# A scan layer with a gated feed-forward: a small early read of w_up on ScalarE's queue, and one store of the last slab whole

## The chip, the cores and the metric

The kernel runs on one core of one Trainium2 chip. The metric is the device time of one execution in microseconds (us); lower is better. The median of three timed runs before the change is 178.91 us (178.73 to 178.92).

## The reference, cut to what matters

The input x has 2048 tokens of 512 features in bf16. It is normalized per token. One branch is a diagonal complex linear recurrence over the tokens, the other a gated feed-forward of width 1376; the output is x plus their product.

```
xn = layernorm(x)
Lam_bar = exp(exp(log_dt) * (Lambda_re + 1j*Lambda_im))
Bu = xn @ B_bar.T                                   # B_bar from Lambda, B_re, B_im
h[t] = Lam_bar * h[t-1] + Bu[t]                     # 512 complex states
s = 2 * real(h @ C.T) + xn * Dskip
g = silu((gelu(xn @ w_gate) * (xn @ w_up)) @ w_down)
out = x + s * g
```

## The kernel before, in words

The tokens are cut into four slabs of 512, each of four tiles of 128 tokens (one per partition). For each slab TensorE forms the gate and up products (`gate_tile`), the down product (`down_pair`), the input product of the recurrence (`half`) and its output product (`y_part`); VectorE runs the recurrence as scans over rotated states, ScalarE moves products out of PSUM with Gelu, Silu or Copy, and SP's queue issues nearly all transfers: loads, transposes by DMA and stores.

The order of the work isn't found at run time. Every step is added to a plan with its reads and writes (`Plan.add`), and `Plan.run` emits the steps in the order of the tuple `ORDER`, written out by step number. Costs, ranks and due times that stand in the calls were a planner's, and decide nothing here. Each engine executes its own instructions in the order in which they were emitted; an instruction that waits holds all that stand behind it on its queue.

The first slab has a way of its own, since its data are still on their way:

- SP issues tiles 0, 1 and 2 of x (L222), then w_up in four quarters of 128 rows by 1024 columns and the rest of its columns in one piece (L213), tile 3 of x, w_gate in two pieces, and later loads.
- ScalarE loads an activation table with a Silu of one element (L254) and issues three small reads of 512 parameters each: log_dt, Lambda_im and Lambda_re (L256).
- TensorE first multiplies constants into banks that are overwritten later (`dummies` L299, `fill` L303).
- Tile 0 of x is summed over its 512 columns by VectorE (384, L341) and ScalarE (128, L339), and centered by VectorE (L343). Tiles 1 and 2 are summed by ScalarE (L347) and centered by VectorE (L348).
- TensorE transposes tile 0 (L313), tile 1 (L328), then the parameters (L603, L604), then begins the product of tile 0 with w_up (L388), transposes tile 2 (L328), and goes on with the product, one quarter of w_up after the other.

The framework gives every transfer that SP or ScalarE issues one of eight completion semaphores, in turn. The issue of a transfer waits, on the queue that issues it, until the transfer that last held the same semaphore has landed. In the built program the turn is not the order of `ORDER` but that in which the framework expects the issues. It begins like this (the number is the semaphore's):

```
0 x tile 0    1 x tile 1    2 x tile 2        3 log_dt
4 w_up 0      5 Lambda_im   6 w_up 1          7 Lambda_re
0 w_up 2      1 w_up 3      2 w_up, rest      3 x tile 3
4 w_gate      5 w_gate      6 w_down, last    7 x slab 1
0 Dskip       1 ...
```

At the other end, the output of a tile is the recurrence's product times g (L502), plus x (L508), and its store is issued from SP (L513). In the last slab the stores of tiles 0 and 1 are cut into two halves of 256 columns each, that of tile 2 is whole, and tile 3 is worked and stored in two halves. The line `cuts` (L511) decides this.

Of the kernel before, what the change touches and what calls it, by code (L numbers as in the profile page):

```python
# [17 lines left out]
PE, ACT, DVE, POOL, SP = "PE", "ACT", "DVE", "POOL", "SP"  # L18


ORDER = (
# [23 lines left out]
)  # L45


# [33 lines left out]
def kernel(  # L81
# [27 lines left out]
    NS = S // TS  # L109
    M = TS // P  # L110
# [4 lines left out]
    HD = D // 2  # L115
# [5 lines left out]
    V, A, G, T = nc.vector, nc.scalar, nc.gpsimd, nc.tensor  # L121
# [6 lines left out]
    def sb(name, shape, dt=BF16):  # L128
        return consts.tile(shape, dt, name=name)
# [49 lines left out]
    def dve(n, emit, reads=(), writes=(), rate=1.0, base=DV, **kw):  # L179
        return pl.add(DVE, base + n / 960.0 / rate, emit, reads, writes, lag=0.13, **kw)  # L180

    def acts(n, emit, reads=(), writes=(), ptr=0, **kw):
        return pl.add(ACT, AC + 0.12 * ptr + n / 1200.0, emit, reads, writes, lag=0.16, **kw)

    def pe(n, cols, emit, reads=(), writes=(), **kw):
        return pl.add(PE, n * (cols + 6) / 2400.0, emit, reads, writes, lag=0.22, **kw)
# [4 lines left out]
    def dma(eng, issue, land, emit, reads=(), writes=(), **kw):  # L191
        return pl.add(eng, issue, emit, reads, writes, lag=land, **kw)
# [43 lines left out]
    for ri, src in enumerate((A_B_re, A_B_im)):  # L236
        dma(SP, 2.0, 3.0, lambda ri=ri, src=src: nc.sync.dma_start_transpose(out=BT[:, ri, :, :], in_=src), writes=[("BT", ri)],
            after=list(sp_last), svc=TURN)
# [13 lines left out]
    one = nc.const_aps.tensor(1.0, [P, 1], FP32)  # L252

    first = [acts(1, lambda: act(out=tiny[:], in_=one, func=AF.Silu), [], ["tiny"], rank=910.0, not_before=0.72)]  # L254
    for i, (t, v) in enumerate(((pv0[0:4, :], A_log_dt), (pv1[0:4, :], A_Lambda_im), (pv1[4:8, :], A_Lambda_re))):
        first = [dma(ACT, 0.48, 1.7, lambda t=t, v=v: A.dma_start(out=t, in_=v.rearrange("(k p) -> k p", p=P)),  # L256
                     writes=[("pv", i)], rank=900.0, not_before=0.8, after=first)]
# [230 lines left out]
    def y_part(s, m, c0, c1, bank, key, seed, e):  # L488

        w = c1 - c0  # L490
        ps = bank[:, 0:w]
        if seed:
            acts(w, lambda: act(out=ps, in_=sk[s % 2][:, m, c0:c1], func=AF.Copy), [("sk", s % 2, m)], [key])  # L493

        def f():
            for j in range(2 * NPT):
                T.matmul(ps, lhsT=hst[s % 2][:, j // NPT, j % NPT, m * P : (m + 1) * P], rhs=C2[:, j // NPT, j % NPT, c0:c1],  # L497
                         start=(j == 0 and not seed), stop=(j == 2 * NPT - 1), skip_group_check=True)
        pe(2 * NPT, w, f, [("hst", s % 2, 0), ("hst", s % 2, 1)] + C2S + ([key] if seed else []), [key])
        gi, b = g2s[s, m]  # L500
        if seed:
            dve(w, lambda: V.tensor_tensor(out=yg[e][:, c0:c1], in0=ps, in1=g2[gi][:, b, c0:c1], op=ALU.mult), [key, ("g2", gi, b)], [("yg", e, c0)])  # L502
        else:
            ys = tF[:, 0, c0:c1]
            dve(w, lambda: V.tensor_tensor(out=ys, in0=ps, in1=sk[s % 2][:, m, c0:c1], op=ALU.add), [key, ("sk", s % 2, m)], [("tF",)])
            dve(w, lambda: V.tensor_tensor(out=yg[e][:, c0:c1], in0=ys, in1=g2[gi][:, b, c0:c1], op=ALU.mult), [("tF",), ("g2", gi, b)], [("yg", e, c0)])
        o = 2 + m % 2 if s == NS - 1 and m >= M - 2 else m % 2
        dve(w, lambda: V.tensor_tensor(out=ot[o][:, c0:c1], in0=yg[e][:, c0:c1], in1=x_tok[:, s * M + m, c0:c1], op=ALU.add),  # L508
            [("yg", e, c0), ("x", s, m)], [("ot", o, c0)], rate=2.0)
        mg = s * TS + m * P  # L510
        cuts = (0, HD) if (NS - 1, 0) <= (s, m) < (NS - 1, M - 2) else (c0,)  # L511
        for lo, hi in zip(cuts, (*cuts[1:], c1)):
            dma(SP, 0.35, 1.5, lambda lo=lo, hi=hi: nc.sync.dma_start(out=out_td[mg : mg + P, lo:hi], in_=ot[o][:, lo:hi]), [("ot", o, c0)], [("out", s, m, lo)], svc=(2, 0.4, 0.9))  # L513

# [218 lines left out]
    for pt in range(NPT):  # L733
# [3 lines left out]
            out=C2[:, 0, pt, :], in0=CT[:, 0, pt, :], scalar=cre[:, pt : pt + 1], in1=tF[:, 1, :], op0=ALU.mult, op1=ALU.subtract),  # L737
            ["coef", ("CT", 0), ("tF",)], [("C2", 0, pt)], base=0.13)
        dve(512, lambda pt=pt: V.scalar_tensor_tensor(
            out=C2[:, 1, pt, :], in0=CT[:, 1, pt, :], scalar=ncre[:, pt : pt + 1], in1=tF[:, 0, :], op0=ALU.mult, op1=ALU.subtract),  # L740
# [104 lines left out]
```

## Time and profile before

| what | us |
|---|---|
| median of three timed runs | 178.91 |
| lowest and highest | 178.73, 178.92 |
| span of the profiled execution | 176.3 |
| median less that span | 2.6 |
| TensorE busy in the span | 172.3 |
| VectorE busy | 156.9 |
| ScalarE busy | 123.5 |

The span runs from the first to the last instruction of the one execution that the profiler recorded; of that execution no other time is given, so the table sets the median of the timed runs beside it. PE stands for TensorE's products, PEld for its loads of weights, DVE for VectorE, ACT for ScalarE, POOL for GpSimd and SP for SyncE; a q behind the name is the engine's queue, where transfers are issued. L with a number is a line of the kernel before. Times of products overlap, since one starts before the last has ended.

### The profile page before, as it was taken

The numbers are of one execution on the slowest core, as the hardware profiler recorded it, in microseconds if no ns is written. First come the engines' busy times: TensorE is split into PE (matmuls) and PEld (weight loads), VectorE is DVE, ScalarE is ACT, GpSimd is POOL, SyncE is SP. The second block draws the span as 40 slices with busy tenths as digits, with TensorE's granted clock in tenths as the row PEclk, the third lists the DMA queues.
The fourth block names the chain that finished last, engine by engine and source line by source line (L and its number), as shares of the span: only waits on it lengthen the run. The fifth ranks groups of instructions, "written<-read, shape, count | busy, mean of one in ns | idle before, by whom it ended". The sixth has DMA issues, their size and how long they took to land.

```text
span 176.3 us, 2421 instructions
## 1 busy us (share of the span) xinstructions
PE 172.3 (98%) x847; PEld 82.3 (47%) x847; DVE 156.9 (89%) x252; ACT 123.5 (70%) x236; POOL 11.2 (6%) x25
## 2 busy tenths in 40 slices
PE   8999999999999999999999999999999999999992
PEld 2555454444454544444455454444444455444451
DVE  3859999999699984999979999899999999999764
ACT  6599979969999999799588845383058518482240
POOL 2660030000200000000040000000000000000000
PEclk9999999999999999999999999999999999999999
DMA  5999999998000809422000084194000007627112
GB/s 156 322 371 225 205 226 260 219 279 137 0 0 12 188 20 192 95 75 46 0 0 6 30 137 95 41 182 86 0 0 0 0 30 162 65 41 154 45 58 76
DMA packets 48355, 18.66 MB, mean 106 GB/s; under 512 B 40312, under 2 KB 47832, under 8 KB 48344
## 3 DMA queue, kind: packets, MB, share of 16 engines
q1 hardware_dynamic: 48320, 18.52, 48.8%
q8 instruction: 6, 0.10, 0.3%
q14 instruction: 5, 0.04, 0.1%
q10 hardware_dynamic: 24, 0.00, 0.0%
HBM read 6.46 MB, written 2.10 MB: 49 GB/s over the span
## 4 chain that ended last, share of the span: by engine, by line
PE 97%; DVE 1%; issue 0%; DVEq 0%
PE ring L449 32%; PE ring L481 22%; PE ring L547 16%; PE ybank L497 15%; PE ring L418 5%; PE ring L388 3%; PE ybank L418 2%; PE ring L299 1%; DVE yg L502 1%; PE ybank L299 1%; DVE junk L508 1%; PE ybank L328 0%; PE ring L303 0%; PE ring L313 0%; PE ring L603 0%
## 5 line engine op out<-in xcount | busy, mean ns | idle before, releaser
L449 PEld LDWEIGHTS <-xnT 128*128 128x128 bf16 x288 | 28.2, 98 | 28.4
L481 PE MATMUL ring<-wd,atT 128*128 128x512 bf16 (+1 forms) x176 | 39.3, 379 | 0.0
L449 PE MATMUL ring<-wg,xnT 128*128 128x512 bf16 (+1 forms) x144 | 31.6, 357 | 0.0
L449 PE MATMUL ring<-wu,xnT 128*128 128x512 bf16 (+1 forms) x144 | 31.3, 357 | 0.0
L547 PE MATMUL ring<-xnT,BT 128*128 128x512 bf16 x128 | 30.1, 379 | 0.0
L578 DVE TENSOR_TENSOR_SCAN Fs<-rho,ini,W 128x512 bf16<-128x512 f32 x24 | 29.7, 1271 | 0.1
L452 ACT ACTIVATE ub<-ring 128x512 bf16<-128x512 f32 (+1 forms) x36 | 19.2, 555 | 13.8 <-PE ring L449 13.7
L497 PE MATMUL ybank<-C,hst 128*128 128x512 bf16 x120 | 27.7, 379 | 0.0
L481 PEld LDWEIGHTS <-atT 128*128 128x128 bf16 (+1 forms) x176 | 17.2, 97 | 20.9
L549 ACT ACTIVATE U<-ring 128x512 bf16<-128x512 f32 x32 | 18.1, 599 | 7.5 <-PE ring L547 7.5
L452 ACT ACTIVATE gt<-ring 128x512 bf16<-128x512 f32 (+1 forms) x36 | 19.5, 556 | 3.7 <-PE ring L449 3.5
L497 PEld LDWEIGHTS <-hst 128*128 128x128 bf16 x136 | 13.3, 98 | 14.0
L484 ACT ACTIVATE g<-ring 128x512 f32<-128x512 f32 x16 | 9.4, 594 | 14.3 <-PE ring L481 14.2
L547 PEld LDWEIGHTS <-BT 128*128 128x128 bf16 x128 | 12.5, 97 | 14.8
L559 DVE TENSOR_TENSOR Q<-U,tab 128x4096 bf16<-128x4096 bf16 x8 | 18.3, 2289 | 0.9 <-ACT tab L646 0.7
L559 DVE TENSOR_TENSOR Q<-Fs,tab 128x4096 bf16<-128x4096 bf16 x8 | 18.3, 2288 | 0.1
L502 DVE TENSOR_TENSOR yg<-ybank,g 128x512 bf16<-128x512 f32 x15 | 10.2, 685 | 5.8 <-PE ybank L497 5.7
L763 ACT ACTIVATE junk<-x_tok 128x512 bf16<-128x512 bf16 x16 | 10.0, 632 | 1.2 <-DMA x_tok<-in_A_x_dram 1.2
L493 ACT ACTIVATE ybank<-sk 128x512 f32<-128x512 bf16 x15 | 9.1, 605 | 1.7 <-DVE yg L502 1.6
L768 ACT ACTIVATE xna<-x_tok,nb,rs 128x512 bf16<-128x512 bf16 x12 | 9.5, 812 | 0.0
L578 DVE TENSOR_TENSOR_SCAN Fs<-rho,W 128x512 bf16<-128x512 f32 x8 | 9.3, 1210 | 0.1
L458 DVE TENSOR_TENSOR at<-gt,ub 128x1024 bf16<-128x1024 bf16 x12 | 8.2, 683 | 0.0
(140 smaller groups left out, 169.7 us busy)
## 6 DMA issues: line engine op xcount, KB each, us to landing
x_tok<-in_A_x_dram SPq DMA_DIRECT2D x3, 512.0 KB, 4.6
out_dram<-ot SPq DMA_DIRECT2D x12, 128.0 KB, 1.8
wd<-in_B_w_down_dram SPq DMA_DIRECT2D x1, 1280.0 KB, 7.1
wu<-in_B_w_up_dram SPq DMA_DIRECT2D x4, 256.0 KB, 3.9
wg<-in_B_w_gate_dram SPq DMA_DIRECT2D x1, 864.0 KB
x_tok<-in_A_x_dram SPq DMA_DIRECT2D x4, 128.0 KB, 2.1
wg<-in_B_w_gate_dram SPq DMA_DIRECT2D x1, 512.0 KB, 6.0
wu<-in_B_w_up_dram SPq DMA_DIRECT2D x1, 352.0 KB, 5.3
```

What stands on the lines that cost most here:

```text
L418: T.matmul(ps[:, 0 : b - a], lhsT=lhs(k), rhs=wt[:, k, a:b], start=(k == 0), stop=(k == KT - 1))
L449: T.matmul(ps[:, 0 : b - a], lhsT=xnT[:, s % 2, m, k, :], rhs=wt[:, k, a:b], start=(k == 0), stop=(k == KT - 1))
L452: acts(b - a, lambda: act(out=dst[:, a:b], in_=ps[:, 0 : b - a], func=AF.Copy if up else AF.Gelu_apprx_tanh), [("bank", r)], [key], table= ...
L481: T.matmul(ps[:], lhsT=atT[:fs, k, m * P : (m + 1) * P], rhs=wd[:fs, k, :], start=(k == 0), stop=(k == NFT - 1))
L497: T.matmul(ps, lhsT=hst[s % 2][:, j // NPT, j % NPT, m * P : (m + 1) * P], rhs=C2[:, j // NPT, j % NPT, c0:c1], start=(j == 0 and not seed ...
L502: dve(w, lambda: V.tensor_tensor(out=yg[e][:, c0:c1], in0=ps, in1=g2[gi][:, b, c0:c1], op=ALU.mult), [key, ("g2", gi, b)], [("yg", e, c0)])
L547: T.matmul(ps[:], lhsT=BT[:, ri, k, pt * P : (pt + 1) * P], rhs=xnT[:, s % 2, :, k, :], start=(k == 0), stop=(k == KT - 1))
L549: acts(512, lambda q=q, ri=ri, ps=ps: act(out=U[ui][:, ri, q, :], in_=ps[:], func=AF.Copy), [("bank", r)], [("U", ui, q, ri)])
L559: dve(4096, lambda: V.tensor_tensor(out=Qf, in0=src.unsqueeze(1).to_broadcast(WQ), in1=table, op=ALU.mult), reads, ["Q"], rate=2.0)
L578: pl.add(DVE, 1.12 if s == 0 else 1.185, lambda ri=ri, q=q, pt=pt, first=first: V.tensor_tensor_scan(out=Fs[:, ri, q, :], data0=rho[:, pt ...
L763: acts(512, lambda i=i, fn=fn, sc=sc, m=m: act(out=junk()[:], in_=x_tok[:, s * M + m, :], func=fn, scale=sc, accum_out=sx[:, s, i, m : m + ...
L768: acts(512, lambda m=m: act(out=xn[m], in_=x_tok[:, s * M + m, :], func=AF.Identity, scale=rs[:, s, m : m + 1], bias=nb[:, s, m : m + 1]), ...
```

## The change

A new step stands between the one-element Silu and the parameters. It reads w_up (512 rows of 1376) at every eighth row, the first 32 columns: 16 partitions with four pieces of 32 bf16 values each, 64 pieces of 64 bytes. Nothing reads the tile that it fills. The condition on the cut of stores now begins at tile 1 of the last slab, so the store of tile 0 is whole. The numbers in `ORDER` are shifted by the new step and by the missing store; otherwise the sequence of steps is the same, with the new step second, behind the Silu.

```
     first = [acts(1, lambda: act(out=tiny[:], in_=one, func=AF.Silu), [], ["tiny"], rank=910.0, not_before=0.72)]
+    seen = sb("seen", [16, 4, 32])
+    first = [dma(ACT, 0.48, 1.7, lambda: A.dma_start(out=seen[:], in_=B_w_up.rearrange("(a b) f -> a b f", a=16)[:, 0:32:8, 0:32]),
+                 writes=["seen"], rank=900.0, not_before=0.8, after=first)]
     for i, (t, v) in enumerate(((pv0[0:4, :], A_log_dt), (pv1[0:4, :], A_Lambda_im), (pv1[4:8, :], A_Lambda_re))):
...
-        cuts = (0, HD) if (NS - 1, 0) <= (s, m) < (NS - 1, M - 2) else (c0,)
+        cuts = (0, HD) if (NS - 1, 1) <= (s, m) < (NS - 1, M - 2) else (c0,)
```

In the built program the semaphores are given in this turn:

```
0 x tile 0    1 x tile 1    2 x tile 2        3 the new read
4 w_up 0      5 log_dt      6 w_up 1          7 Lambda_im
0 Lambda_re   1 w_up 2      2 w_up 3          3 w_up, rest
4 x tile 3    5 w_gate      6 w_gate          7 w_down, last
0 x slab 1    1 Dskip       2 ...
```

The last transfers, from the halves of tile 1 on, have the same semaphores as before.

46 rows, old and new, of the table ORDER are left out of this document.

## The prediction, as it stood before the result

> **What bounds the kernel now.** I read the page's busy shares and its chain first, then the busy time by stretches, then the order of time up to 6 us and from 169 us. The page:
>
> ```profile
> PE 172.3 (98%) x847; PEld 82.3 (47%) x847; DVE 156.9 (89%) x252; ACT 123.5 (70%) x236; POOL 11.2 (6%) x25
> ...
> PE 97%; DVE 1%; issue 0%; DVEq 0%
> ```
>
> TensorE is busy 98% of the span and makes up 97% of the chain that ended last. The busy time by stretches (stretch, its length, then busy time and count of each engine) tells where the other few per cent lie:
>
> ```profile
> 5.00:30.00 25.00, 25.00 (x131) 12.43 (x130) 22.13 (x64) 21.00 (x41) 7.19 (x14) 1.00 1.09 274
> 30.00:60.00 30.00, 30.00 (x149) 14.28 (x147) 27.96 (x39) 27.85 (x56) 1.01 (x1) 1.00 0.61 115
> ...
> 150.00:171.30 21.30, 21.30 (x102) 9.81 (x101) 18.34 (x23) 9.84 (x19) 0.00 (x0) 1.00 0.37 71
> 171.30:176.30 5.00, 1.75 (x17) 1.32 (x14) 2.37 (x6) 0.00 (x0) 0.00 (x0) 1.00 0.26 79
> ```
>
> In the stretches shown up to 171.30 TensorE's busy time equals the length to the last digit, at the full granted clock (1.00). So from 5 us on nothing is waited for, and the end is the moment at which this unbroken run begins, plus a constant, plus the tail. The change touches exactly these two ends: the first 5 us, and stores of the last slab. What sets the beginning is in the chain by pieces and in the order of time (start, length, engine, line; in brackets the idle time before and what ended it):
>
> ```profile
> 4.50 0.40 PE ybank L328 x4
> 4.90 0.11 PE ring L603
> 5.01 0.03 PE ring L604
> 5.03 0.55 PE ring L388 x2
> ```
>
> ```profile
> 0.72 1.28 ACT L254 ACT_TABLE_LOAD   x1 [0.72 <-PEq L829]
> 0.79 0.55 ACTq L256 DMA_DIRECT2D pv<-in_A_log_dt_dram  x1
> 1.38 0.26 ACTq L256 DMA_DIRECT2D pv<-in_A_Lambda_im_dram  x1
> 1.66 0.31 ACTq L256 DMA_DIRECT2D pv<-in_A_Lambda_re_dram  x1
> 2.85 0.31 ACT L339 ACTIVATE junk<-x_tok 128x128 bf16<-128x128 bf16 x1 [0.63 <-DMA x_tok<-in_A_x_dram]
> 3.06 0.19 ACT L339 ACTIVATION_READ_ACCUMULATOR junk<-x_tok 128x1 f32 x1
> 3.33 0.63 ACT L347 ACTIVATE junk<-x_tok 128x512 bf16<-128x512 bf16 x1
> 3.52 0.41 DVE L343 TENSOR_SCALAR xna<-x_tok,ma,mb 128x512 bf16<-128x512 bf16 x1
> 3.87 0.19 ACT L347 ACTIVATION_READ_ACCUMULATOR junk<-x_tok 128x1 f32 x1
> 3.96 0.63 ACT L347 ACTIVATE junk<-x_tok 128x512 bf16<-128x512 bf16 x1
> 4.09 0.35 DVE L348 TENSOR_SCALAR xna<-x_tok,ma 128x512 bf16<-128x512 bf16 x1 [0.16 <-ACT junk L347]
> 4.50 0.23 PEld L328 LDWEIGHTS <-xna 128*128 128x128 bf16 x4 [0.23 <-DVE xna L348]
> 4.83 0.17 PE L603 MATMUL ring<-ident,pv 4*128 4x4 bf16 x1
> 5.65 4.91 PE L388 MATMUL ring<-wu,W 128*128 128x512 bf16 x22
> ```
>
> The reader is to see one path: tile 1 of x lands, ScalarE sums it (L347, 3.33), VectorE centers it (L348, 4.09), TensorE transposes it (L328, 4.50), then the parameters (L603, L604), then the first product with w_up (L388, 5.03). L328 is the last place at which the weight queue waited (0.23). The first quarter of w_up must be there for L388 too. The issues on SP's queue and the time to landing of single loads (the last number) say whether it is:
>
> ```profile
> 0.72 1.34 SPq L222 DMA_DIRECT2D x_tok<-in_A_x_dram  x3
> 2.11 2.33 SPq L213 DMA_DIRECT2D wu<-in_B_w_up_dram  x5
> 4.49 0.50 SPq L222 DMA_DIRECT2D x_tok<-in_A_x_dram  x1
> 5.04 1.49 SPq L213 DMA_DIRECT2D wg<-in_B_w_gate_dram  x2
> ```
>
> ```profile
> x_tok<-in_A_x_dram SPq DMA_DIRECT2D x1, 128.0 KB, 2.1
> ```
>
> ```profile
> wu<-in_B_w_up_dram SPq DMA_DIRECT2D x1, 256.0 KB, 2.8
> ```
>
> ```profile
> wu<-in_B_w_up_dram SPq DMA_DIRECT2D x1, 256.0 KB, 3.3
> ```
>
> ```profile
> wu<-in_B_w_up_dram SPq DMA_DIRECT2D x1, 256.0 KB, 4.5
> ```
>
> x tile 0 is issued at 0.72 and lands 2.1 later, at 2.82. The first quarter of w_up is issued at 2.11 and lands at 4.91, ahead of its use at about 5.0 by a tenth or less. Issues of w_up are 0.47 apart (2.33 for five), so the second goes out at 2.58 and lands at 5.88, needed at 5.65 + 2 x 0.216 = 6.08 (a product takes 4.75 / 22 = 0.216 in the chain; 4.91 here counts the last one's tail). The third goes out at 3.05 and lands at 7.55, needed after ten products at 7.81. So w_up is near the limit three times, and late nowhere.
>
> **The change part by part.** *The read itself.* It is the first transfer on ScalarE's queue, so the three parameter reads move back by one place. It moves 64 x 64 bytes = 4 KB, against 128 KB of the tile of x that is under way. Nobody waits for its data. If its purpose is that later reads of w_up start faster, the gain is bounded: DMA rates are
>
> ```profile
> 3.30:4.10 0.80, 0.80 (x5) 0.23 (x4) 0.53 (x4) 0.77 (x3) 0.00 (x0) 1.00 0.89 247
> 4.10:5.00 0.90, 0.90 (x13) 0.55 (x12) 0.82 (x4) 0.90 (x4) 0.00 (x0) 1.00 1.00 319
> ```
>
> 247 GB/s while w_up starts and 319 after. The loss is 0.80 x (1 - 247/319) = 0.18 us, which I take as the most that the stream of w_up can come forward. TensorE has at most about 0.1 to gain from it, and only if tile 1 of x comes earlier too, since L328 to L604 fill 4.50 to 5.03. I count it at 0.
>
> *ScalarE's queue.* Each issue of the parameters takes 0.26 to 0.55; the read's own I put at the first one's 0.55 (bounds 0.26 and 0.55). Before, the third issue ended at 1.66 + 0.31 = 1.97. Alone, the shift would end at most at 2.5, still ahead of 2.85, where ScalarE stood idle for x (0.63). That cover is enough.
>
> But the read also takes one of the eight completion semaphores. In the changed order x tile 0, 1, 2, read, w_up 0, log_dt, w_up 1, Lambda_im come first, and the ninth, Lambda_re, is given the semaphore of x tile 0: its issue waits on ScalarE's queue for that tile, up to 2.82. Behind it stand the summing of tile 0 (L339) and of tile 1 (L347). Lambda_re's issue, 0.31 long, now lies between 2.85 and 3.16, and L339 starts 0.31 to 0.34 later with the step between two instructions. L347 of tile 1 had stood until 3.33 for its tile (x issues are 1.34 / 3 = 0.45 apart, so tile 1 is issued at 1.17 and lands at about 3.3); it can follow L339 by 3.96 - 3.87 = 0.09 after the start of the accumulator's reading. That start goes from 3.06 to 3.40, so L347 starts at 3.49 to 3.50 in place of 3.33: 0.16 to 0.17 later. L343 (3.52) needs tile 0's sum, which was ready at 3.25 and now is at 3.59: about 0.1 later, less than the other path. L348, L328, L603 and L388 all follow L347 by fixed steps: **+0.17**. If the issue takes only 0.26, it is +0.12; if 0.55, +0.41; I take 0.31, the same transfer's own row.
>
> The Trainium skill, DMA: Bandwidth & Descriptors, Anatomy of one DMA, says that a transfer's semaphore wait is done by the issuing sequencer before dispatch, not by the DMA engines. No run here shows a held issue on ScalarE's queue yet. By that rule the 0.17 stands; if the engines waited instead, the term would be nothing.
>
> *The parameters.* Lambda_re now leaves at 2.85. Its landing time isn't in the views; the nearest are 2.1 for 128 KB of x and 1.5 for the small stores below, so it lands between 4.35 and 4.95. L604 needs it, now at 5.0 + 0.17. It is in time, with 0.2 left at worst.
>
> *SP's queue.* The same turn of the semaphores makes w_up 2 wait for x tile 1 (about 3.3, issue before 3.05), w_up 3 for x tile 2 (1.61 + 2.1, about 3.7, before 3.52), and x tile 3 for w_up 0 (4.91, before 4.49); the gate's two issues follow. They leave 0.3 to 0.5 later. Their landings are 4.5 us after issue, since the engines work off what is queued (share 1.00 in the row above), so I expect no later landing. If the third quarter slipped by its whole 0.3, from 7.55 to 7.85, TensorE, itself 0.17 later, would ask for it at 7.98. Nothing is paid at either end. From the second slab of x on each transfer waits for the same one as before.
>
> *x behind the read.* The 64 pieces go out beside x tile 0. At least 0 (4 of 132 KB); at most the 0.18 lost at the start of w_up, if that loss moves to the front. I take 0.07: **+0.07**.
>
> *The store.* Whole instead of halves takes one issue from SP near 169:
>
> ```profile
> 169.13 0.33 SPq L513 DMA_DIRECT2D out_dram<-ot  x1
> ```
>
> ```profile
> 173.91 0.33 SPq L513 DMA_DIRECT2D out_dram<-junk  x1
> ```
>
> ```profile
> out_dram<-junk SPq DMA_DIRECT2D x2, 64.0 KB, 1.5
> ```
>
> The tail hangs on the last store, issued at 173.91 and landed at about 175.4. The changed store is 4.78 earlier, and one landing (1.5) doesn't reach that far. With one transfer more in front and one less here, the last six have the semaphores they had. Cost and gain 0.
>
> *The sum:* 0.17 + 0.07 = +0.24 on the span, 176.3 to 176.5. The profiled execution's span and the median of the timed runs differ by 178.91 - 176.3 = 2.6, which lies around the span and doesn't change: **179.15 us**.
>
> **The rivals.** *A, x is held up by the read (slower).* If each of the four pieces of an engine (64 over 16) costs the whole 0.18 in turn, x lands 0.72 later; if two do, 0.36. With the 0.17 that gives +0.5 to +0.9, 179.4 to 179.8. Against it: the pieces of the parameters go out in the same time, and tile 0 of x still lands in the 2.1 quoted. For it: pieces of a cold tensor haven't been put ahead of x before. It decides from about 0.2 us of delay of tile 0 on. Beside it, the skill (same page, Issuing engines are not separate DMA queues; Bandwidth) says that both queues' transfers interleave on the same 16 engines and gives 0.68 us for 4 KB in 64 packets: an estimate by that page is +0.17 + 0.68 = +0.85. No row here shows such a transfer.
>
> *B, Lambda_re lands late.* If it comes 0.4 later than the upper end of 4.95, behind w_up's packets, L604 waits to 5.35 instead of 5.17: +0.42 with the x term, 179.3. For it: the engines are full from 4.10 on. Against: 1 KB, and its own queue.
>
> *C, w_up gates in the timed runs (faster).* The margins are a tenth, 0.2 and 0.26. If an execution without the profiler loses more at the start of w_up than this one, TensorE waits there for two or three of the quarters, ScalarE's 0.17 hides under that wait, and the read takes away 0.18 or twice that, up to 0.5: 178.4 to 178.7. Against it: the profiled execution shows no wait at all there, and the three runs lie within 0.2.
>
> *The read warms nothing.* Then the forecast stands unchanged, as I count no gain.
>
> **How the numbers follow.** Forecast (+0.12 to +0.41) 0.45; A 0.25; B 0.10; C 0.20. What a measurement of this kernel can tell from no change is about 0.2%, 0.36 us. The forecast lies within it but for a small part; A is beyond it, B half; C is half beyond, but other causes of a gain that I don't see are added there. So faster 0.19, same 0.43, slower 0.38. The range takes in the forecast, B, C from 178.5 and A to 179.8.
>
> **What would show it.** In the changed profile: Lambda_re's issue at about 2.85 and ScalarE's first activation on x at about 3.2; L347's successor at 3.5; the transposes of tile 1 at 4.67; the first product at 5.2; stretches from there to the end of the run again full; the last store about 0.24 later. I am wrong if ScalarE isn't held behind tile 0, if tile 0 lands later than 3.0 (A), if TensorE idles between tile 1's transposes and the parameters' (B), or if the first product starts before 5.0 (C).

## The result, and the profile after

| | us |
|---|---|
| changed kernel, median of 13 executions | 179.14 (178.56 to 181.11) |
| kernel before, median of 13 beside it | 178.76 (178.03 to 180.90) |
| difference of the medians | +0.38 |
| ratio, 95% interval | 1.0047 (1.0025 to 1.0070) |

The change makes the kernel slower by a little. Three executions of the changed kernel and two of the kernel before took about 181 us, and so did one, two and three in the runs below with one piece and the hold, without the hold, and with C_re: without all of these the means differ by +0.36 (0.06 to 0.67), +0.32, +0.42 and +0.69, while the ratio of 1.0047 is near that of the means (1.0045) only if the two are left out and the three are counted. The argument below rests on the medians and the profiles.

The page of the changed kernel, span 177.2 us against 176.3:

```profile
PE 171.7 (97%) x831; PEld 82.5 (47%) x847; DVE 157.0 (89%) x252; ACT 123.7 (70%) x236; POOL 11.3 (6%) x25
...
PE 93%; DMA 2%; DVE 1%; SPq 1%; issue 1%; DVEq 0%
```

TensorE has gone from 97% of the chain to 93%, and DMA and SP's queue are in it, which they weren't. That isn't 4% of time lost: the chain now runs back from the first product through the flight of w_up's first quarter to SP's issues. Its pieces up to there (start, length, what):

```profile
1.64 0.60 SPq L222
...
2.29 3.58 DMA wu<-in_B_w_up_dram
...
5.91 0.59 PE ring L391 x2
```

The count of products, 831 in place of 847, isn't work that went away: nine of the thirteen profiles here lack 16 records of products, while the loads of weights are 847 in this page and in that of before, and the missing time shows as small gaps. What came late is in the order of time (start, length, engine, line; in brackets the idle time before and what ended it). First one line of the kernel before, its first product, then the changed kernel:

```profile
5.00 0.59 PE L388 MATMUL ring<-wu,W 128*128 128x512 bf16 x2
```

```profile
0.72 1.52 SPq L222 DMA_DIRECT2D x_tok<-in_A_x_dram  x3
0.79 0.71 ACTq L256 DMA_DIRECT2D seen<-in_B_w_up_dram  x1
1.53 0.73 ACTq L259 DMA_DIRECT2D pv<-in_A_log_dt_dram  x1
2.29 2.95 SPq L213 DMA_DIRECT2D wu<-in_B_w_up_dram  x5
2.29 0.26 ACTq L259 DMA_DIRECT2D pv<-in_A_Lambda_im_dram  x1
2.94 0.25 ACTq L259 DMA_DIRECT2D pv<-in_A_Lambda_re_dram  x1
3.24 0.31 ACT L342 ACTIVATE junk<-x_tok 128x128 bf16<-128x128 bf16 x1 [1.02 <-DMA x_tok<-in_A_x_dram]
3.45 0.19 ACT L342 ACTIVATION_READ_ACCUMULATOR junk<-x_tok 128x1 f32 x1
3.74 0.63 ACT L350 ACTIVATE junk<-x_tok 128x512 bf16<-128x512 bf16 x1
4.90 0.40 PE L331 MATMUL ybank<-ident,xna 128*128 128x128 bf16 x4 [0.25 <-DVE xna L351]
5.57 0.17 PE L607 MATMUL ring<-ident,pv 8*128 8x8 bf16 x1 [0.17 <-DMA pv<-in_A_Lambda_re_dram]
5.91 0.59 PE L391 MATMUL ring<-wu,W 128*128 128x512 bf16 x2 [0.16 <-DMA wu<-in_B_w_up_dram]
```

The lines of the code are 3 higher than before. Three things are late, one behind the other: tile 1's transposes (L331, 4.90 against 4.50), then Lambda_re (L607), then the first quarter of w_up (L391). The first product starts at 5.91 in place of 5.00 (5.03 by the chain): +0.91, and the span is 0.9 longer. The issues on both queues have grown too: three tiles of x take SP 1.52 in place of 1.34, nearly all of it in the third (0.60 above, 0.42 before), so w_up leaves at 2.29 and not at 2.11; the read takes ScalarE 0.71, and log_dt behind it 0.73, where it took 0.55 as the first and the second issue 0.26. The time from issue to landing of single loads:

```profile
seen<-in_B_w_up_dram ACTq DMA_DIRECT2D x1, 4.0 KB, 2.3
...
wu<-in_B_w_up_dram SPq DMA_DIRECT2D x1, 256.0 KB, 3.6
x_tok<-in_A_x_dram SPq DMA_DIRECT2D x1, 128.0 KB, 2.8
```

The first quarter of w_up lands 3.6 after its issue, at about 5.88; it was 2.8 and 4.9. (The tile of x in the last row is tile 2.) Behind the start nothing has changed. The stretches (length, then busy time and count of PE, PEld, DVE, ACT, POOL, then the granted clock, DMA share and rate):

```profile
5.91:30.00 24.09, 23.98 (x123) 12.04 (x125) 21.32 (x62) 19.72 (x39) 7.33 (x14) 1.00 1.13 268
...
172.20:177.20 5.00, 1.78 (x17) 1.34 (x14) 2.37 (x6) 0.00 (x0) 0.00 (x0) 1.00 0.26 79
```

TensorE is full but for the missing records, and the last 5 us are those of before (1.75 there). SP's last stores, of the kernel before and of the changed one:

```profile
165.93 5.67 SPq L513 DMA_DIRECT2D out_dram<-ot  x6
172.59 1.65 SPq L513 DMA_DIRECT2D out_dram<-junk  x3
```

```profile
166.85 5.67 SPq L516 DMA_DIRECT2D out_dram<-ot  x5
173.51 1.65 SPq L516 DMA_DIRECT2D out_dram<-junk  x3
```

Both groups begin 0.92 later and last as long. So the end is the start plus a constant: 176.3 - 5.00 = 171.3 before, 177.2 - 5.91 = 171.3 after. The profiled execution of the changed kernel took 179.01 in all, 1.8 more than its span. A time of these two is therefore the moment of the first product plus 173.1. If that holds in the executions without a profile too, the median of 178.76 means a start at 5.66, and 179.14 one at 6.04.

### The profile page after: what moved, and what is told of

The parts are those of the page before. It is cut to its first block, busy times and chain, and to the rows that moved or that the text cites. A ratio compares the mean times of both kernels' runs of the same rounds, so it can differ in the third digit from the quotient of the medians.

```text
span 177.2 us, 2405 instructions
## 1 busy us (share of the span) xinstructions
PE 171.7 (97%) x831; PEld 82.5 (47%) x847; DVE 157.0 (89%) x252; ACT 123.7 (70%) x236; POOL 11.3 (6%) x25
## 4 chain that ended last, share of the span: by engine, by line
PE 93%; DMA 2%; DVE 1%; SPq 1%; issue 1%; DVEq 0%
PE ring L452 31%; PE ring L484 21%; PE ring L550 16%; PE ybank L500 14%; PE ring L421 5%; PE ring L391 3%; PE ybank L421 2%; DMA wu<-in_B_w_up_dram 2%; SPq L222 1%; DVE yg L505 1%; DVE junk L511 1%; PE ybank L331 0%; DVEq L505 0%
```

## The experiments

All were compared on medians with the kernel before beside them (178.63 of 29 executions in the first group, 178.54 of 18 in the second, 178.71 of 23 in the third), and each has a profile. The runs that are compared have 12 executions each, that with C_re 11, with 16 pieces 7 and the last 6. The hold is ScalarE's wait for tile 0 of x, which Lambda_re's issue makes; the pieces are the 64 separate runs of 64 bytes of the new read.

**The kernel before, twice more.** No edit. On record for the first and for the second:

> The kernel before once more, one look, for a second profile of its first 6 us. The first profile of it had its first product with w_up at 5.03 and a span of 176.3, while the median of its timed runs is 2.5 above that span. If the start is steady, the first product begins between 5.0 and 5.1 again and the quarter of w_up lands about 2.8 after its issue. If the start varies from execution to execution, the first product begins anywhere from 5.0 to 5.8 and the landing of w_up moves with it, and a single profile of either kernel may not be set against another without that scatter.

> The kernel before once more, for the spread of its start on this chip: first product between 5.0 and 5.5, set by the landing of the first quarter of w_up (4.9 to 5.5); span 176.3 to 177.0.

They took 178.49 (span 176.7) and 178.72 (176.9). For each, the first product from the order of time, and the first quarter of w_up from the times to landing:

```profile
5.39 0.59 PE L388 MATMUL ring<-wu,W 128*128 128x512 bf16 x2 [0.18 <-DMA wu<-in_B_w_up_dram]
```

```profile
wu<-in_B_w_up_dram SPq DMA_DIRECT2D x1, 256.0 KB, 3.2
```

```profile
5.67 0.59 PE L388 MATMUL ring<-wu,W 128*128 128x512 bf16 x2 [0.59 <-DMA wu<-in_B_w_up_dram]
```

```profile
wu<-in_B_w_up_dram SPq DMA_DIRECT2D x1, 256.0 KB, 3.5
```

The issue stands at 2.11 in all three profiles of this kernel, and the landing comes 2.8, 3.2 or 3.5 later. In the two new ones TensorE had tile 1 and the parameters transposed at 5.2 and 5.1 and stood waiting for w_up (0.18 and 0.59 in the brackets). The profile on which the prediction was built, 176.3 + 1.8 = 178.1, was among the shortest executions of this kernel (178.03 is the shortest in its comparison), the one in which w_up happened to come just in time. The traces also record sixteen completion signals for each quarter, and the last of them is the landing. In the three profiles the first signal comes at 4.57, 4.54 and 4.47 and the eighth at 4.70, 4.71 and 4.75, but the last at 4.95, 5.34 and 5.62: what varies is when a few late parts of the load arrive.

**The store alone.** The diff of `cuts`, without the read.

> Only the second edit: the store of tile 0 of the last slab whole, no new read. Theory of the prediction: the store is off the path that sets the end, so the ratio is 1.000 within 0.001 or so, the first product begins at 5.0 to 5.1 as before, and the last store leaves 174.0 - 173.9 = 0 later. Rival: the store's semaphores or its 128 KB in one piece hold something in the tail; then the ratio is 1.001 to 1.003 and the last store leaves 0.2 to 0.5 later relative to the end of the products.

178.75 against 178.63, ratio 1.0012 (1.0000 to 1.0024); first product at 5.40. At most 0.24%, and hardly that: a later run that has the same store (one piece in log_dt's place, below) stands at +0.02. The store is not where the time went.

**The read without the hold.** log_dt's read is left out, its tile filled with a constant, so that the number of transfers is that of before and ScalarE waits for no turn (the filling and the shifted numbers are left out here):

```
-    for i, (t, v) in enumerate(((pv0[0:4, :], A_log_dt), (pv1[0:4, :], A_Lambda_im), (pv1[4:8, :], A_Lambda_re))):
+    for i, (t, v) in enumerate(((pv1[0:4, :], A_Lambda_im), (pv1[4:8, :], A_Lambda_re))):
```

> The read of 64 pieces takes the place of the read of log_dt, which is left out (its tile is set to -2 by VectorE), so that ScalarE again issues three transfers and the turn of the semaphores is that of before: no issue waits for tile 0 of x. Theory of the hold (ScalarE held behind tile 0): the loss is gone, first activation on x at 2.85 to 2.95, first product at 5.0 to 5.2, ratio 0.999 to 1.001. Rival, the pieces themselves (their issue and their packets push tile 1 and 2 of x and w_up back): tile 1 lands 2.5 after its issue, the first quarter of w_up 3.3 to 3.6 after its own, first product at 5.5 to 5.9, ratio 1.003 to 1.005. Both together in the changed kernel gave 1.0047.

179.19 against 178.63: +0.56, ratio 1.0045 (1.0018 to 1.0073), as much as the whole change. From its order of time:

```profile
0.79 0.71 ACTq L256 DMA_DIRECT2D seen<-in_B_w_up_dram  x1
...
2.85 0.31 ACT L342 ACTIVATE junk<-x_tok 128x128 bf16<-128x128 bf16 x1 [0.64 <-DMA x_tok<-in_A_x_dram]
...
3.73 0.63 ACT L350 ACTIVATE junk<-x_tok 128x512 bf16<-128x512 bf16 x1 [0.48 <-DMA x_tok<-in_A_x_dram]
...
6.11 0.59 PE L391 MATMUL ring<-wu,W 128*128 128x512 bf16 x2 [0.68 <-DMA wu<-in_B_w_up_dram]
```

ScalarE begins on tile 0 at 2.85 as before, so the hold is gone. But tile 1 lets ScalarE begin only at 3.73, in place of 3.3 to 3.5 in the profiles of before (it idles 0.48), and TensorE idles 0.68 for w_up, which landed at about 6.07, 3.8 after its issue. The theory on which the prediction stood, that the hold is the cost, falls here: without it a loss of the same size is there.

**The hold without the pieces.** The read is one piece of 64 bytes; the turn of the semaphores is that of the change:

```
-    first = [dma(ACT, 0.48, 1.7, lambda: A.dma_start(out=seen[:], in_=B_w_up.rearrange("(a b) f -> a b f", a=16)[:, 0:32:8, 0:32]),
+    first = [dma(ACT, 0.48, 1.7, lambda: A.dma_start(out=seen[0:1, 0, :], in_=B_w_up[0:1, 0:32]),
```

> The changed kernel with the read cut from 64 pieces to one (row 0, 32 columns): the turn of the semaphores and the place on ScalarE's queue stay, the pieces go. Theory of the hold: Lambda_re still leaves only after tile 0 of x, at about 2.9, ScalarE's first activation on x starts at about 3.2, tile 1's sum at 3.5, Lambda_re lands after 5.0, first product at 5.2 to 5.6, ratio 1.001 to 1.003. Rival, the pieces: with one piece nearly all of the loss is gone, tile 1 lands 2.1 and w_up 2.8 after issue, first product within 0.2 of before, ratio 1.000 to 1.001.

178.98 against 178.63: +0.35, ratio 1.0025 (1.0000 to 1.0049).

```profile
2.85 0.26 ACTq L259 DMA_DIRECT2D pv<-in_A_Lambda_re_dram  x1
3.15 0.31 ACT L342 ACTIVATE junk<-x_tok 128x128 bf16<-128x128 bf16 x1 [0.93 <-DMA x_tok<-in_A_x_dram]
...
5.27 0.17 PE L607 MATMUL ring<-ident,pv 8*128 8x8 bf16 x1
5.38 0.60 PE L391 MATMUL ring<-wu,W 128*128 128x512 bf16 x2
```

The hold is exactly where the prediction put it: Lambda_re at 2.85, the first activation on x at 3.15. In this execution (178.45, the second shortest of its 12) w_up landed 2.8 after its issue, so the start isn't set by it. It is set by Lambda_re: L607 follows L606 (5.08) by 0.19, where L604 followed L603 by 0.04 in the order of time before (4.83, 4.87), and the trace has the last signal of Lambda_re at 5.22, 2.4 after its held issue. In the kernel before it came at 3.48, 1.8 after its issue. The sum of tile 1 begins at 3.58, but tile 1 itself had landed only at 3.56; the hold would have let it begin at 3.45. So the hold costs by the parameter that leaves late, not by the sums. A start of 5.38 lies below the 5.53 that the median beside it means (178.63 - 173.1), so at this landing it should cost little. The median says +0.35, with an interval that touches none; Lambda_re comes later still in the runs with the hold and more pieces (5.34 to 6.07), which may be where those lie, but no profile of this run shows it.

**Neither.** One piece in the place of log_dt's read, filled as above.

> The read is one piece of 64 bytes in place of the read of log_dt (whose tile is filled with a constant), so it neither moves any transfer's turn nor holds ScalarE; the store is whole. If the number of pieces ahead of x and w_up is what costs: as with the store alone, ratio 1.000 to 1.002, ScalarE's sum of tile 1 from 3.4 to 3.6, first product 5.0 to 5.4. If any further tensor touched ahead costs, one piece too: ratio 1.003 to 1.005 and a first product at 5.6 or later, behind a landing of the first quarter of w_up at 5.6 or later. If the hold made the 1.0025 seen with one piece and the hold: this one is 0.2 to 0.4 us below that one.

178.73 against 178.71: +0.02, ratio 1.0004 (0.9990 to 1.0019), and a first product at 5.33. With it the four corners stand: neither +0.02; the hold alone +0.35; the pieces alone +0.56; both, the change, +0.38. The medians don't add up, and a reason is at hand: the start is the later of two arrivals, w_up's, which the pieces move, and that of x and the parameters, which the hold moves (and the pieces, through tile 1). But the intervals of the three that lose overlap, so that the two costs don't add up is argued, not shown.

**The same pieces from another tensor.** C_re is read in place of w_up, in the same 64 pieces; the changed kernel was run once beside it.

```
-    ... in_=B_w_up.rearrange("(a b) f -> a b f", a=16)[:, 0:32:8, 0:32]),
+    ... in_=A_C_re.rearrange("(a b) f -> a b f", a=16)[:, 0:32:8, 0:32]),
```

> The changed kernel with the 64 pieces taken from C_re, which is used only much later, in the same shape, at the same place. Theory of the pieces (the cost is their number on the way, wherever they come from): as the changed kernel, issue of the read 0.7, tile 1 of x landing 2.4 to 2.6 after issue, first product at 5.7 to 6.1, ratio 1.003 to 1.006. Rival, the rows of w_up (reading w_up early gets in the way of its own first quarter, or speeds it up): without it w_up's first quarter lands at another time than in the changed kernel by 0.2 or more, and the ratio leaves 1.003 to 1.006 on that side.

> The changed kernel once more, one look, for a second profile of its first 6 us. If the later start is the change's and not one execution's, tile 1 of x lands again 2.4 to 2.6 after its issue, w_up's first quarter 3.3 to 3.8 after its own, and the first product begins at 5.7 to 6.1, against 5.39 in the second profile of before. If it was chance, the first product begins at 5.0 to 5.5.

179.56 against 178.54: +1.02, ratio 1.0063 (1.0035 to 1.0091). The changed kernel took 178.99 (span 177.2). There w_up landed 3.5 after its issue, before TensorE asked for it, and the path of tile 1 ended last, with transposes that took 0.61 in place of 0.40 (on this see the last section):

```profile
4.03 0.63 ACT L350 ACTIVATE junk<-x_tok 128x512 bf16<-128x512 bf16 x1 [0.43 <-DMA x_tok<-in_A_x_dram]
5.20 0.61 PE L331 MATMUL ybank<-ident,xna 128*128 128x128 bf16 x4 [0.27 <-DVE xna L351]
...
5.87 0.61 PE L391 MATMUL ring<-wu,W 128*128 128x512 bf16 x2
```

With C_re's pieces:

```profile
4.02 0.63 ACT L350 ACTIVATE junk<-x_tok 128x512 bf16<-128x512 bf16 x1 [0.39 <-DMA x_tok<-in_A_x_dram]
...
6.13 0.59 PE L391 MATMUL ring<-wu,W 128*128 128x512 bf16 x2 [0.28 <-DMA wu<-in_B_w_up_dram]
```

```profile
wu<-in_B_w_up_dram SPq DMA_DIRECT2D x1, 256.0 KB, 3.8
```

The last row is the first quarter of w_up again, 3.8 after its issue. The loss is there whichever tensor is read. That w_up's own rows do less harm than C_re's would be a small gain from touching them. The rival's terms on record are just met (the quarter lands 0.2 to 0.3 later than in the two profiles of the changed kernel, and the ratio is above 1.006), but with w_up's rows and without the hold the quarter came as late, and the intervals overlap, so it is neither shown nor excluded.

**The same 4 KB in 16 pieces.** 16 rows of w_up, 256 bytes of each (`B_w_up[0:512:32, 0:128]`), the hold kept.

> The changed kernel with the same 4 KB of w_up in 16 pieces of 256 bytes instead of 64 of 64 (every 32nd row, first 128 columns), one piece on each engine. Theory of the pieces' number: the read's issue falls from 0.71 towards 0.55, the next issue on ScalarE from 0.73 to 0.3, that of tile 2 of x from 0.60 to 0.43, w_up's first quarter is issued at 2.1 again and lands before 5.5, first product at 5.3 to 5.5, ratio 1.000 to 1.003. Rival, that any read on all 16 engines ahead of x tile 1 costs this, whatever its pieces: first product at 5.7 or later and ratio 1.003 to 1.005.

179.42 against 178.54: +0.88, ratio 1.0041 (1.0026 to 1.0055).

```profile
0.79 0.40 ACTq L256 DMA_DIRECT2D seen<-in_B_w_up_dram  x1
...
5.18 0.63 ACT L350 ACTIVATE junk<-x_tok 128x512 bf16<-128x512 bf16 x1 [1.01 <-DMA x_tok<-in_A_x_dram]
...
6.12 0.17 PE L607 MATMUL ring<-ident,pv 8*128 8x8 bf16 x1 [1.00 <-DMA pv<-in_A_Lambda_re_dram]
```

The issue is short again (0.40), SP's issues are back at 1.34 and w_up leaves at 2.11, but still takes 3.6 to land. Tile 2 of x keeps ScalarE idle for 1.01, and Lambda_re keeps TensorE idle for 1.00: issued at 2.85, it lands 3.2 later. Of tile 2's sixteen signals fifteen had come by 3.93; the last came at 5.09. The theory of the pieces' number, which expected 5.3 to 5.5, fails, and the rival on record, that any read over all engines ahead of tile 1 costs this, has its terms met (first product at 6.22). The long issues are thus not the whole of it: in this profile too something behind the early read is late, here the tile and the parameter, there tile 1 and w_up. Two things stay untested. The single piece moves 64 bytes and not 4 KB, so number, spread over engines and bytes aren't told apart. And the interval overlaps that of the single piece with the hold, so how much of the +0.88 is the pieces' and how much the hold's isn't settled.

**The read, later.** The same 64 pieces, issued by ScalarE behind its sums of tiles 1 and 2.

> The same 64 pieces, but issued by ScalarE behind its sums of tiles 1 and 2 of x, at about 4.6, so the parameters leave as in the kernel before and ScalarE isn't held; the store is whole. If the pieces cost only because they go ahead of x and the first quarter of w_up: ratio 1.000 to 1.002, first product 5.0 to 5.4, no wait for later quarters. If 64 pieces cost wherever they meet w_up's transfers: 0.2 to 0.7 us of waits of TensorE for the second to fourth quarter, ratio 1.002 to 1.005. If a read of w_up's rows ahead of need helped later quarters, it would be below the store alone (1.0012).

178.92 against 178.71: +0.21, ratio 1.0005 (0.9988 to 1.0022): no loss that can be told.

```profile
4.20 0.66 ACTq L259 DMA_DIRECT2D seen<-in_B_w_up_dram  x1
...
5.30 0.59 PE L391 MATMUL ring<-wu,W 128*128 128x512 bf16 x2
...
7.32 4.48 PE L391 MATMUL ring<-wu,W 128*128 128x512 bf16 x20 [0.77 <-DMA wu<-in_B_w_up_dram]
```

The start is at 5.30. The profiled execution (179.30) was the longest of the 12: it waited 0.77 for the second quarter, which had been issued at about 2.6, well before the read. One such wait in one profile doesn't tell whether the pieces caused it; the median says that they mostly don't. The position matters, then: at the head of the queue the pieces stand at +0.38 with the hold and +0.56 without, behind the first sums at +0.21, which the interval can't tell from nothing.

**A try for something faster.** No read; tile 1 of x goes first on ScalarE's queue instead, so that w_up leaves SP earlier. The parameters' transposes stand behind the first products, and one step of POOL is moved ahead (the changes of `ORDER` are left out here).

```
-        dma_sp(end, landed, lambda: nc.sync.dma_start(out=x_tok[:, m, :], in_=x_r[:, m, :]), [("x", 0, m)])
+        q = A if m == 1 else nc.sync
+        dma_sp(end, landed, lambda: q.dma_start(out=x_tok[:, m, :], in_=x_r[:, m, :]), [("x", 0, m)])
```

> The kernel before with no extra read, and with ScalarE's queue used for what the start waits for: tile 1 of x is issued first on ScalarE's queue instead of second on SP's, so that tile 2 and w_up move forward by one issue (0.47) on SP. The transposes of the parameters move behind the first products, since Lambda_re now leaves later, and one step of POOL moves ahead of the power that needs the parameters. If the first quarter of w_up sets the start (it did at 5.39 in the second profile of before), it is issued at 1.65, lands at 4.5 to 4.9, and the first product begins at 4.9 to 5.1: ratio 0.997 to 0.999. Rival, that transfers issued close together only share the same way in: w_up lands at 5.3 as before and the ratio is 1.000 to 1.002.

179.31 against 178.54: +0.77, ratio 1.0035 (1.0017 to 1.0053).

```profile
1.65 4.91 SPq L213 DMA_DIRECT2D wu<-in_B_w_up_dram  x5
...
3.29 0.26 ACTq L257 DMA_DIRECT2D pv<-in_A_Lambda_re_dram  x1
...
6.18 0.59 PE L389 MATMUL ring<-wu,W 128*128 128x512 bf16 x2 [0.65 <-DMA wu<-in_B_w_up_dram]
```

```profile
wu<-in_B_w_up_dram SPq DMA_DIRECT2D x1, 256.0 KB, 4.5
```

w_up left 0.46 earlier, took 4.5 to land in place of 2.8 to 3.5, and came later than ever. Sending it sooner did not bring it sooner here. The hold is in this kernel too (Lambda_re leaves at 3.29), but TensorE waited for w_up. No run here beat the kernel before.

## Why the prediction was right, and where not

The time and the sign came out: 179.15 forecast, 179.14 measured; +0.24 forecast, +0.38 between the medians. The way there was mostly another, and the profile misses the marks that were set for it: the first product at 5.91 and not 5.2, tile 1's transposes at 4.90 and not 4.67, the last store 0.92 later and not 0.24, and TensorE waits for Lambda_re (0.17 at L607), which is the sign of rival B.

- **"From 5 us on nothing is waited for": right, counted from the first product.** Span less first product is 171.2 to 171.4 in ten of the thirteen profiles, the changed kernel's among them. The three others are one with slower first products (172.0, last section), one that waited for a later quarter (172.2), and the one with tile 1 on ScalarE's queue (171.7), where the parameters' transposes stand behind the first product.
- **The store at 0: right** within 0.24%, from the store alone; the tail has the length of before.
- **ScalarE held behind tile 0: right as a mechanism.** Forecast 2.85 and about 3.2; 2.94 and 3.24 in the changed kernel, 2.85 and 3.15 with one piece. The Trainium skill, DMA: Bandwidth & Descriptors, Anatomy of one DMA, says that the issuing sequencer and not the DMA engine does the waiting; these rows agree, since ScalarE's activation stands behind the held issue. The path by which it should cost, through the sum of tile 1, set no start here. Only with 16 pieces does that sum begin where the hold puts it (3.46); with 64 pieces, or one, it waits for tile 1 itself. So the +0.17 was reached by a path that didn't count. The hold's cost in the profile with one piece goes through Lambda_re (first product at 5.38, ahead of w_up in a usual execution, which would hide it); by the median it is +0.35, by its interval anything from none to +0.9.
- **"It is in time, with 0.2 left at worst": wrong.** Lambda_re, forecast to land at 4.35 to 4.95, landed at 5.22 with one piece, and released L607 at 5.57 in the changed kernel and at 6.12 with 16 pieces. Its 1 KB took 2.4, 2.6 and 3.2 from its issue, longer than the 128 KB of x that I had taken as the upper bound. In the changed kernel's trace its four packets of 256 bytes ran from 4.53 on, 1.3 after its issue had ended (0.9 at most in the kernel before), and took 15 to 18 ns each: the time went by before them, while w_up's packets ran. Rival B's place was real, if not the main one.
- **x behind the read, +0.07: the term that was mis-sized.** The pieces alone cost +0.56. They do it in three places: ScalarE gets tile 1 of x at 3.73 to 4.03, w_up is issued 0.16 to 0.18 later, and it takes 3.5 to 3.8 to land in place of 2.8 to 3.5. The eighth of w_up's sixteen signals comes at 4.91 to 5.10 in place of 4.70 to 4.75, the last at 5.75 to 6.09 in place of 4.95 to 5.62: again the last parts lose most. The prediction priced only bytes, for tile 0, the one transfer that was not late (2.85 without the hold). It took the issue's own length, 0.55 where it was 0.71, as free under cover, and didn't see that other issues grow with it: SP's three tiles by 0.18, and the second one on ScalarE from 0.26 to 0.73. Rival A, x held up by the read, was right about the read and wrong about the tile; its price by the piece isn't borne out, since 16 pieces cost no less.
- **Issues that lengthen each other.** With a read of 0.71 on ScalarE, SP's three issues go from 1.34 to 1.52; with reads of 0.40 to 0.52 (16 pieces or one) they take 1.34 to 1.42. The Trainium skill, Perfetto Trace Analysis, DMA Instruction — HWDGE (DVE, Sync), says that the block that generates descriptors is shared by two sequencers, that it is locked for one at a time, and that waiting for that lock is inside the issue's recorded length; which two engines issue such transfers it calls the compiler's choice. By that rule a longer issue on one queue lengthens those that meet it on the other, and the trace agrees by the lengths just given.
- **"w_up is near the limit three times, and late nowhere": right for that execution, wrong for the kernel**, and the deepest of the errors, since it came from one execution. In the two other profiles of before, TensorE waited for the first quarter, 0.18 and 0.59. The 2.6 between the median and that profile's span, "which lies around the span", is 1.8 around it and 0.8 of a later start. Rival C's condition thus held: w_up gates in the timed runs. Its consequence didn't: the read doesn't take that wait away, it lengthens it, whether it reads w_up or C_re.
- **Why the number was still right.** By luck: errors met. The hold was counted in full and the pieces at almost nothing, where the medians give the pieces the larger part and the two together no more than one of them; and the sum was added to a median of three, 178.91, where 13 executions gave 178.76. The span of the profile grew by 0.9, not 0.24; the medians grew by less, since the first profile of before was one of its shortest.

What stays open: why the last signals of w_up come up to 0.7 apart in the same program, why a single piece with the hold has a median of +0.35, and why a read of 4 KB makes parts of the loads behind it late.

## What to carry to other kernels

When the bound is one transfer at the start, ask several executions how late it comes before you price anything against its margin, and know the whole time of the profiled execution beside its span (1.8 more here), or the difference to the median is misread, as it was. A transfer put ahead of it can cost far more than its share of the bytes (4 KB beside tiles of 128 KB: +0.56): by its place in the line, by its issue, which lengthened those on the neighbouring queue, and by parts of the loads behind it that come late. A short issue alone didn't save it. And where delays lie on paths that meet, price each against the later arrival.

## What the hardware did that I had not expected

A read of 4 KB with 64 pieces takes 0.66 to 0.71 to issue, one with 16 pieces 0.40, one with a single piece 0.51 to 0.52, the last two at the head of the queue. The issue behind it takes 0.73 after 64 pieces, 0.57 after 16, and 0.25 to 0.26 after one.

In the profile of one piece in log_dt's place, TensorE took 1.6 to 1.75 times as long for its first products. The views give a granted clock of 1.00 from 5 us on, but the trace's record of that clock begins only at 6.63 in this execution, and the views count the time ahead of it as 1.00:

```profile
4.62 0.63 PE L331 MATMUL ybank<-ident,xna 128*128 128x128 bf16 x4
...
5.33 1.03 PE L391 MATMUL ring<-wu,W 128*128 128x512 bf16 x2
6.16 0.62 PE L331 MATMUL ybank<-ident,xna 128*128 128x128 bf16 x4
```

The same four transposes take 0.40 in the changed kernel, and two products 0.59. The three groups lose 0.23 + 0.44 + 0.23 = 0.9, of which 0.67 falls behind the first product: its span, 177.3, is just that much more than 5.33 + 171.3. It isn't this program's alone. In five other traces the record begins at 4.30, 4.62, 4.88, 5.17 and 5.74, and there the transposes start about 0.11 apart ahead of it and about 0.055 behind it; here the first two products start 0.40 apart, and 0.21 apart from 6.83 on. So up to that moment TensorE ran at about half its later rate in these executions. In the second profile of the changed kernel (5.74) this is why the four transposes took 0.61, ahead of the first product; in the first profile of the kernel before the record begins at 4.03, ahead of the transposes of tile 1. So the start has one more source of scatter than w_up's landing. What decides when the record begins isn't shown here.
